# Softmax of the later attention tiles head by head on ScalarE, and the quarter-product weights formed at other places of a one-core kernel

## The chip, the core and the metric

The kernel runs on one core of one Trainium2 chip. The metric is the time of one launch in device microseconds, the median of some runs. One execution was taken by the hardware profiler, and all rows below are of that one.

## The reference

Everything is float32. The input is attention over independent chunks of 64 positions (8 batches, 8 heads, 576 positions, 64 numbers each), then two layers over 4608 tokens:

```python
scores = scale * np.matmul(q_c, k_c.transpose(0, 1, 2, 4, 3))   # 64 x 64 per chunk
attn = np.exp(scores - np.max(scores, axis=-1, keepdims=True))
attn = attn / (np.sum(attn, axis=-1, keepdims=True) + 1e-09)
x = np.matmul(attn, v_c)                                        # laid out as 4608 x 512
x = softplus(x @ w_in) @ w_out                                  # 512 -> 2048 -> 512
h = np.maximum(np.maximum(x @ w1, x @ w2), x @ w3)              # 512 -> 768
out = h @ w_out2                                                # 768 -> 512
```

The weights come as float64 and are split on the chip into float32 parts.

## The kernel before, in words

**Blocks and tiles.** The 4608 tokens are 9 blocks of 512. A block has 4 attention tiles (two heads each), 36 in all. Tiles 0 to 7 are made by `attention_first`, tiles 8 to 35 by `attention`, which is the function that the change is about. A float32 matmul is done in three passes over a high and a low part, so each operand is split: a cast makes the high part (g or s), and a subtraction on VectorE makes the low one (`cut_up`, or the pair `copy_op` and `tt_op`; on the profile lines 281, 283 and 288, which are the helpers).

**Stages.** Blocks 0 to 2 go through the first layer in plain steps (`mlp1`). Blocks 3 to 8 go in three pairs: `strassen()` runs eight `UnitA` per pair, each of seven half-size products p1 to p7 where eight would be plain, and then the second half of the layer, the outs. For pairs 0 and 1 these are `mlp1_out` steps of both blocks (the block that comes later reloads its g from DRAM, `tmp<-gd`), for pair 2 the quarter products of `Sevens.step` (steps p = 5, 6, 3, 4, 7, four each). The last layers are three `Triple`, each of 15 products per width (`product`, line 1558) and the outs (line 1656).

**What `attention` does for a tile.** It loads q and k in a shape that VectorE can transpose (lines 689 and 690), and v. A group of 64x64 matmuls makes the scores of this tile and the weighted sum of an older one. For 14 tiles (8 to 21) the group stands among the `mlp1` steps and writes the PSUM tile `aps`. For the other 14 (22 to 35, `apart`) it stands behind p7 of a unit (line 588 on the profile) and writes the two banks X and Z (`one` on the profile), which p2, and p5 and p3, of the units write too. Then comes `softmax`: the maximum of each head's 64 scores (line 545 or 563), the subtraction (line 288, `p<-one,mx` or `p<-aps,mx`), one activation over 512 numbers (line 579; Softplus with a shift of -20 stands for the exponential), the sums (line 580), two tiny operations, the division, a transpose (line 742), and a trip through DRAM (`pd`).

**Weights.** `combos` forms the weights of the quarter products: from four wide weight tiles of the first layer it makes four sums and four combinations, splits each combination, and stores them with six GpSimd DMAs into `wso`. It is called four times, for n2 = 0 to 3. `weights3(late)` does the like for the Triples, with stores into `w2c`, and `Triple.product` loads them (line 1541). `againa` loads the unit weights (`s<-wac`, line 1034).

**What sets the order.** All engines run lists that `Plan.order` writes before the launch: it takes every operation with its cost per engine and its due time (an operation without one gets the earliest of those that need it, less their cost), and at each moment gives an idle engine the ready operation that is due first. So an engine's list is fixed, and an operation that waits holds up all behind it on that engine. The matmuls of the pairs are chained in program order (`in_line("h", ...)`), so their order is fixed by the program. GpSimd (POOL) and SyncE (SP) issue most DMAs and also work through fixed lists.

The places where the change acts are `softmax` (line 535), its call in `attention` (line 739), `put` in `weights3` (line 903), the table `COMBOS` (line 977), the gate of the `w2c` loads (line 1544) and the calls of `combos` (line 1771):

```python
COMBOS = (1, 4, 7, 10)          # after which outs of pair 0
MORE = (3, 0), (5, 0), (5, 0)   # after which steps of the quarter products
```

Of the kernel before, what the change touches and what calls it, by code (L numbers as in the profile page):

```python
# [10 lines left out]
F32 = mybir.dt.float32  # L11
# [3 lines left out]
AF = mybir.ActivationFunctionType  # L15
# [5 lines left out]
P = 128  # L21
# [162 lines left out]
def tile_kernel(ctx: ExitStack, tc: tile.TileContext, q, k, v, w_in, w_out, w1, w2, w3, wo2, out):  # L184
# [350 lines left out]
    def softmax(sc, pbuf, by_head=False):  # L535
# [4 lines left out]
        if sc is None:  # L540
            s3 = lambda e: XZ.t[e][:, :TB // 2].rearrange("p (c k) -> p c k", k=CH)
            for h in range(2):
# [6 lines left out]
                )  # L549
            for h in range(2):  # L550
# [10 lines left out]
        else:  # L561
            s4 = lambda: sc.t[:, :, :TB // 2].rearrange("p e (c k) -> p e c k", k=CH)
            op({"D": 0.69}, lambda e: nc.vector.reduce_max(m4(), s4(), axis=AX.X), r=[(sc, "s")], w=[mx], alloc=[mx, sm])
            if by_head:
                op({"D": 0.1}, lambda e: nc.vector.tensor_scalar(mx.t, mx.t, -SCALE, -DROP, ALU.mult, ALU.add), w=[mx])

                def heads(e):
                    for u in range(H):
                        nc.scalar.activation(
                            p3()[:, u], s4()[:, u // HP, u % HP], AF.Softplus, bias=mx.t[:, u:u + 1], scale=SCALE  # L570
                        )

                op({"A": 1.9}, heads, r=[(sc, "s"), mx], w=[pbuf], alloc=[pbuf])
            else:
                tt_op(
                    p4, s4, lambda: m4()[:, :, :, None].to_broadcast([P, 2, HP, CH]), ALU.subtract, [(sc, "s"), mx], [pbuf], alloc=[pbuf]
                )
        if not by_head:
            op({"A": 0.62}, lambda e: nc.scalar.activation(pbuf.t, pbuf.t, AF.Softplus, bias=drop[:, :1], scale=SCALE), w=[pbuf])
        op({"D": 0.69}, lambda e: nc.vector.reduce_sum(sm.t, p3(), axis=AX.X), r=[pbuf], w=[sm])  # L580
# [95 lines left out]
    def attention(t, after=(), apart=False):  # L676
# [62 lines left out]
        softmax(None if apart else G, pbuf)  # L739
# [131 lines left out]
    def weights3(late, after):  # L871
# [31 lines left out]
        def put(s, r):  # L903
# [9 lines left out]
            tt_op(lo, view(r), lambda: hi().bitcast(F32), ALU.subtract, keys(r) + [(zs[0], "h")], [(zs[-1], "l")], n=n1, hold=[token])  # L913
# [63 lines left out]
    COMBOS = (1, 4, 7, 10)  # L977
# [114 lines left out]
    class UnitA:  # L1092
# [88 lines left out]
        def p3(u):  # L1181
            u.product(3, lambda: two("Z", TB), False, w=[(XZ, "Z")])
            u.add("Z", 0, 1)
# [295 lines left out]
    class Triple:  # L1479
# [47 lines left out]
        def product(u, s, d, alloc=()):  # L1527
# [8 lines left out]
            else:  # L1536
                zs, rings = [slot("w", "x") for _ in range(1 + late)], [Buf("ringb") for _ in range(1 + late)]
                for k, z in enumerate(zs):
# [5 lines left out]
                        after=[store["c", s, late + k], mark["step", *MORE[0]]],  # L1544
# [145 lines left out]
    def strassen():  # L1690
# [19 lines left out]
        for q in range(pairs):  # L1710
# [7 lines left out]
            for n, m in enumerate(ORDER[q]):  # L1718
# [3 lines left out]
                mark["unit", q, n] = begin  # L1722
                if n == SEVENS_LOAD and sevens:
                    mark["sevens", q] = begin
# [43 lines left out]
            for j in range(NJ - 2):  # L1768
                o = out()
                if q == 0 and j in COMBOS:  # L1770
                    combos(COMBOS.index(j), [o], clock[0] + 15.0)
# [113 lines left out]
```

## Time and profile before

| what | value |
|---|---|
| median of 3 runs (lowest, highest) | 1369.16 us (1365.87, 1371.52) |
| the profiled execution, its own time | 1368.65 us |
| its span | 1366.8 us |
| TensorE matmul busy (PE) | 1331.3 us, 97% |
| VectorE busy (DVE) | 1002.6 us, 73% |
| ScalarE busy (ACT) | 505.8 us, 37% |
| GpSimd busy (POOL) | 323.9 us, 24% |
| mean granted TensorE clock | 0.996 of full speed |

The span runs from the first to the last instruction; the time of the launch has 1.85 us around it. A share of busy time is a mean over stages that have different limits. The matmuls take nearly the whole span, so what can be gained is what stands between them.

### The profile page before, as it was taken

The numbers are of one execution on the slowest core, as the hardware profiler recorded it, in microseconds if no ns is written. First come the engines' busy times: TensorE is split into PE (matmuls) and PEld (weight loads), VectorE is DVE, ScalarE is ACT, GpSimd is POOL, SyncE is SP. The second block draws the span as 40 slices with busy tenths as digits, with TensorE's granted clock in tenths as the row PEclk, the third lists the DMA queues.
The fourth block names the chain that finished last, engine by engine and source line by source line (L and its number), as shares of the span: only waits on it lengthen the run. The fifth ranks groups of instructions, "written<-read, shape, count | busy, mean of one in ns | idle before, by whom it ended". The sixth has DMA issues, their size and how long they took to land.

```text
span 1366.8 us, 22719 instructions
## 1 busy us (share of the span) xinstructions
PE 1331.3 (97%) x8616; PEld 1091.1 (80%) x8616; DVE 1002.6 (73%) x1551; ACT 505.8 (37%) x793; POOL 323.9 (24%) x568
## 2 busy tenths in 40 slices
PE   5899999999999999999999999999999999999998
PEld 3788888888888778777788887888888888888886
DVE  8999976797676998658958897879714597145951
ACT  4544333354433544335535553432123222132211
POOL 2011545542233324323231122121101122011100
PEclk9899999999999999999999999999999999999999
DMA  8655567676788999887886799655644465344301
GB/s 273 172 165 156 126 194 202 192 261 212 202 246 258 286 327 294 266 282 257 337 296 223 249 345 364 232 192 208 212 149 162 139 231 202 143 147 154 139 30 63
DMA packets 220253, 293.56 MB, mean 215 GB/s; under 512 B 121984, under 2 KB 147008, under 8 KB 220144
## 3 DMA queue, kind: packets, MB, share of 16 engines
q0 software_dynamic: 54400, 180.31, 38.3%
q1 hardware_dynamic: 164928, 111.02, 27.0%
q8 instruction: 68, 1.11, 0.3%
q10 hardware_dynamic: 816, 0.79, 0.2%
q14 instruction: 41, 0.34, 0.1%
HBM read 198.71 MB, written 93.32 MB: 214 GB/s over the span
## 4 chain that ended last, share of the span: by engine, by line
PE 86%; DMA 6%; DVE 5%; SPq 2%; issue 1%; ACT 0%; POOL 0%; DVEq 0%; ACTq 0%; POOLq 0%
PE acc L1558 14%; PE both L1558 13%; PE acc L816 9%; PE acc L1410 9%; PE ph L796 9%; PE ph L1109 8%; PE one L1109 6%; PE both L1656 6%; PE acc L1656 5%; PE acc L1330 2%; PE acc L1263 2%; DVE s L288 2%; DMA rk<-in_k_dram 1%; PE ph L1330 1%; PE aps L503 1%
## 5 line engine op out<-in xcount | busy, mean ns | idle before, releaser
L288 DVE TENSOR_TENSOR s<-s,s 128x1024 fp32r<-128x1024 f32 (+3 forms) x216 | 208.7, 990 | 24.9 <-ACT s L281 11.7
L1410 PE MATMUL acc<-g,s 128*128 128x512 f32 x768 | 184.8, 393 | 3.7 <-DVE g L288 3.7
L1410 PEld LDWEIGHTS acc<-g,s 128*128 128x128 f32 x768 | 142.6, 188 | 35.8 <-DVE g L288 5.8
L1109 PE MATMUL ph<-s,s 128*128 128x512 f32 x576 | 144.3, 390 | 3.0 <-DMA s<-wac 2.1
L796 PE MATMUL ph<-s,s 128*128 128x512 f32 x576 | 141.2, 396 | 0.0
L816 PE MATMUL acc<-g,s 128*128 128x512 f32 x576 | 139.6, 391 | 0.0
L1109 PEld LDWEIGHTS ph<-s,s 128*128 128x128 f32 x576 | 107.9, 188 | 26.2 <-DMA s<-wac 2.6
L796 PEld LDWEIGHTS ph<-s,s 128*128 128x128 f32 x576 | 108.8, 190 | 23.4
L816 PEld LDWEIGHTS acc<-g,s 128*128 128x128 f32 x576 | 107.4, 188 | 22.7
L1541 POOL DMA_DIRECT2D s<-w2c x105 | 55.9, 532 | 278.1 <-PE both L1558 87.5
L281 ACT CAST g<-s 128x1024 fp32r<-128x1024 f32 (+1 forms) x68 | 62.2, 914 | 159.8 <-PE both L1558 36.3
L1558 PE MATMUL acc<-s,s 128*128 128x512 f32 x452 | 120.3, 389 | 0.0
L281 ACT CAST s<-s 128x512 fp32r<-128x512 f32 (+1 forms) x100 | 82.1, 832 | 91.5 <-DVE s L288 32.2
L1558 PE MATMUL acc<-g,s 128*128 128x512 f32 x400 | 110.0, 389 | 0.0
L1109 PE MATMUL one<-s,s 128*128 128x512 f32 x432 | 106.6, 390 | 1.2 <-DVE tmp L288 0.7
L1558 PE MATMUL both<-s,s 128*128 128x512 f32 x400 | 106.3, 389 | 0.0
L1558 PE MATMUL both<-g,s 128*128 128x512 f32 x368 | 100.1, 389 | 0.0
L1558 PEld LDWEIGHTS acc<-s,s 128*128 128x128 f32 x452 | 84.9, 188 | 17.6
L1109 PEld LDWEIGHTS one<-s,s 128*128 128x128 f32 x432 | 80.9, 188 | 19.1 <-DVE tmp L288 1.5
L288 DVE TENSOR_TENSOR g<-tmp,g 128x512 fp32r<-128x512 f32 x104 | 71.1, 684 | 33.2 <-ACT g L281 33.1
L468 POOL DMA_DIRECT2D rv<-in_v_dram x102 | 62.1, 613 | 115.4 <-issue 53.6
L1558 PEld LDWEIGHTS both<-s,s 128*128 128x128 f32 x400 | 75.1, 188 | 15.6
(157 smaller groups left out, 2103.9 us busy)
## 6 DMA issues: line engine op xcount, KB each, us to landing
s<-w2c POOLq DMA_DIRECT2D x105, 512.0 KB, 4.4
s<-wac POOLq DMA_DIRECT2D x66, 512.0 KB, 6.5
w2c<-s POOLq DMA_DIRECT2D x45, 512.0 KB, 4.3
wac<-s POOLq DMA_DIRECT2D x24, 512.0 KB, 5.6
s<-wso SPq DMA_DIRECT2D x20, 512.0 KB, 7.2
s<-in_moe_w_dram POOLq DMA_DIRECT2D x18, 512.0 KB, 4.9
s<-x2d POOLq DMA_DIRECT2D x18, 512.0 KB, 5.6
s<-in_moe_w_in_dram SPq DMA_DIRECT2D x16, 512.0 KB, 5.1
```

What stands on the lines that cost most here:

```text
L281: nc.scalar.copy(dst(), src())
L288: return op({"D": 0.69 * n}, lambda e: nc.vector.tensor_tensor(dst(), a(), b(), f), r=r, w=w, **kw)
L468: dma(out=dst().rearrange("p (c e d) -> p c e d", e=2, d=D)[half * CH:(half + 1) * CH, lo:lo + mine, h, :], in_=v[b, t % HP * 2 + h].rearr ...
L796: nc.tensor.matmul(ph.t, w[:, wi, kk * P:(kk + 1) * P], x[kk].t[:, xi], start=(kk == 0 and wi == 0 and xi == 0), stop=(kk == KD - 1 and wi ...
L816: nc.tensor.matmul(acc[m // 2].t[:, m % 2], w[:, wi, m * P:(m + 1) * P], g.t[:, gi, :], start=(first and wi == 0 and gi == 0), stop=(last ...
L1109: nc.tensor.matmul(dst(), ws.t[:, wi, col + kk * P:col + (kk + 1) * P], x[kk].t[:, xi], start=(first and kk == 0 and wi == 0 and xi == 0), ...
L1263: nc.tensor.matmul(u.acc[f].t[:, m], w.t[:, wi, m * P:(m + 1) * P], g.t[:, gi, :], start=(first and wi == 0 and gi == 0), stop=(last and w ...
L1330: nc.tensor.matmul(dst(m), z.t[:, wi, nn * HT + m * P:nn * HT + (m + 1) * P], (GH, GL)[gi].t[:, nn], start=(fresh and nn == 0 and wi == 0 ...
L1410: nc.tensor.matmul(acc[half].t[:, m % 2], w.t[:, wi, m * P:(m + 1) * P], g.t[:, gi, :], start=(first and wi == 0 and gi == 0), stop=(last ...
L1541: lambda e, k=k, z=z: nc.gpsimd.dma_start(out=z.t.bitcast(F32), in_=w2c[s][late + k]),
L1558: nc.tensor.matmul(bank.view()[:, f], ws(wi, slice(f * HT + kk * P, f * HT + (kk + 1) * P)), (XH, XL)[xi].t[:, kk], start=(first and kk == ...
L1656: nc.tensor.matmul(banks[t // 2].view()[:, t % 2], (GH, GL)[gi].t[:, f, t * P:(t + 1) * P], wo2_of[j].t[:, wi], start=(j == 0 and wi == 0 ...
```

## The change

There are five edits.

1. `softmax` gets a switch `sums`, and `attention` calls it with `by_head` and `sums` on. For tiles 8 to 35 the subtraction and the sums on VectorE go. A tiny operation scales the maxima, and eight activations of 64 numbers read the scores straight from PSUM, take the maximum off as their bias, and give the sum of their row as a second output. `attention_first` is called as before.
2. `combos` is called behind the out 2 of pair 0 (n2 = 0) and behind the first product of the units 0, 3 and 6 of pair 1 (n2 = 1, 2, 3), where all four stood behind the outs 1, 4, 7 and 10 of pair 0. Its due time is 30 us behind the call instead of 15.
3. The low parts in `weights3(0)` get a due time of their own.
4. The `w2c` loads of the first Triple from product 2 on wait for the first step of quarter product 7, not of 3.
5. The planner's cost of the activations is 2.6 with sums, 1.9 without.

```diff
-    def softmax(sc, pbuf, by_head=False):
+    def softmax(sc, pbuf, by_head=False, sums=False):
...
+            r = [(XZ, "X"), (XZ, "Z")]
+            one = lambda u: s3(u // HP)[:, u % HP]
+        else:
+            s4 = lambda: sc.t[:, :, :TB // 2].rearrange("p e (c k) -> p e c k", k=CH)
+            op({"D": 0.69}, lambda e: nc.vector.reduce_max(m4(), s4(), axis=AX.X), r=[(sc, "s")], w=[mx], alloc=[mx, sm])
+            r = [(sc, "s")]
+            one = lambda u: s4()[:, u // HP, u % HP]
+        if by_head:
+            op({"D": 0.1}, lambda e: nc.vector.tensor_scalar(mx.t, mx.t, -SCALE, -DROP, ALU.mult, ALU.add), w=[mx])
+
+            def heads(e):
+                for u in range(H):
+                    nc.scalar.activation(
+                        p3()[:, u],
+                        one(u),
+                        AF.Softplus,
+                        bias=mx.t[:, u:u + 1],
+                        scale=SCALE,
+                        accum_out=sm.t[:, u:u + 1] if sums else None,
+                    )
+
+            op({"A": 2.6 if sums else 1.9}, heads, r=[*r, mx], w=[pbuf, sm] if sums else [pbuf], alloc=[pbuf])
+        elif sc is None:
...
-        op({"D": 0.69}, lambda e: nc.vector.reduce_sum(sm.t, p3(), axis=AX.X), r=[pbuf], w=[sm])
+        if not sums:
+            op({"D": 0.69}, lambda e: nc.vector.reduce_sum(sm.t, p3(), axis=AX.X), r=[pbuf], w=[sm])
...
-        softmax(None if apart else G, pbuf)
+        softmax(None if apart else G, pbuf, True, True)
...
-            tt_op(lo, view(r), lambda: hi().bitcast(F32), ALU.subtract, keys(r) + [(zs[0], "h")], [(zs[-1], "l")], n=n1, hold=[token])
+            tt_op(lo, view(r), lambda: hi().bitcast(F32), ALU.subtract, keys(r) + [(zs[0], "h")], [(zs[-1], "l")], n=n1, hold=[token], due=None if late else T0 + STEP * NJ * (NP + 4))
...
-    COMBOS = (1, 4, 7, 10)
+    COMBOS = (("out", 0, 2), ("unit", 1, 0), ("unit", 1, 3), ("unit", 1, 6))
+    LATER = (7, 0)
...
-                        after=[store["c", s, late + k], mark["step", *MORE[0]]],
+                        after=[store["c", s, late + k], mark["step", *(MORE[0] if s < 2 or u.q else LATER)]],
...
+                if ("unit", q, n) in COMBOS:
+                    combos(COMBOS.index(("unit", q, n)), [begin], clock[0] + 30.0)
...
-                if q == 0 and j in COMBOS:
-                    combos(COMBOS.index(j), [o], clock[0] + 15.0)
+                if ("out", q, j) in COMBOS:
+                    combos(COMBOS.index(("out", q, j)), [o], clock[0] + 30.0)
```

How the lists move. On the engines' lists the lines of the changed kernel carry its own line numbers (9 or 10 higher behind `softmax`). The matmul list is the same row by row up to the first `mlp1` steps, and all of its later differences are places of 64x64 groups among the steps and, in the quarter products, other tiles for the same factors.

VectorE, in the outs of pair 0 behind the score group of unit 7. Before (s_244 and s_245 are the sums of `combos` for n2 = 1, tmp_78 its first combination, g the low parts that the outs wait for):

```order
L288 TENSOR_TENSOR p_89<-one_4129,mx_71 128x256
L288 TENSOR_TENSOR s_244_5634<-s_57_1342 128x512
L288 TENSOR_TENSOR p_89<-one_4130,mx_71 128x256
L288 TENSOR_TENSOR s_244_5634<-s_67_1536 128x512
L288 TENSOR_TENSOR s_245_5635<-s_62_1448 128x512
L288 TENSOR_TENSOR s_245_5635<-s_72_1602 128x512
L288 TENSOR_TENSOR g_77<-tmp_85,g_77 128x512
L288 TENSOR_TENSOR tmp_78<-s_244_5634,s_245_5635 128x512
```

The same outs in the change, up to where the sums for n2 = 1 (here s_250) begin:

```order
L288 TENSOR_TENSOR g_77<-tmp_83,g_77 128x512
L698 STREAM_TRANSPOSE s_248_5860<-rq_74 128x512
L288 TENSOR_TENSOR g_76<-tmp_86,g_76 128x512
L288 TENSOR_TENSOR g_75<-tmp_82,g_75 128x512
L288 TENSOR_TENSOR g_77<-tmp_80,g_77 128x512
L288 TENSOR_TENSOR g_76<-tmp_85,g_76 128x512
L288 TENSOR_TENSOR s_250_5918<-s_57_1342 128x512
```

The combinations for n2 = 1 now stand behind the last low parts of these outs; those for 2 and 3 stand among the units of pair 1. Between the two additions of p2 and p5 that enclose these outs VectorE's list had 78 operations and now has 58.

VectorE again, the score group behind unit 4 of pair 1. Before (`one_4129` and `one_4130` are the banks X and Z):

```order
L545 TENSOR_REDUCE mx_73<-one_4129 128x4
L689 STREAM_TRANSPOSE s_299_6651<-rq_74 128x512
L545 TENSOR_REDUCE mx_73<-one_4130 128x4
L288 TENSOR_TENSOR p_89<-one_4129,mx_73 128x256
L690 STREAM_TRANSPOSE s_299_6651<-rk_87 128x512
L288 TENSOR_TENSOR p_89<-one_4130,mx_73 128x256
```

Now (line 558 is the tiny operation, behind which ScalarE reads both banks):

```order
L698 STREAM_TRANSPOSE s_293_6754<-rq_74 128x512
L545 TENSOR_REDUCE mx_73<-one_4215 128x4
L288 TENSOR_TENSOR g_75<-tmp_81,g_75 128x512
L545 TENSOR_REDUCE mx_73<-one_4216 128x4
L332 TENSOR_SCALAR tmp_78<-s_287_6655 128x512
L558 TENSOR_SCALAR mx_73<-mx_73 128x8
L699 STREAM_TRANSPOSE s_293_6754<-rk_87 128x512
```

The transpose of k no longer stands ahead of the last operation on VectorE that the banks need.

GpSimd, in the quarter products. Before (`w2c_0_183`, `186`, `189` ... are the loads of products 0, 1, 2 ...):

```order
L1541 DMA s_461_8500<-w2c_0_183 128x1024
L917 DMA w2c_1_187<-s_462_8503 128x1024
L917 DMA w2c_2_188<-s_463_8504 128x1024
L1541 DMA s_467_8544<-w2c_0_186 128x1024
L1541 DMA s_471_8569<-w2c_0_189 128x1024
L1541 DMA s_475_8602<-w2c_0_192 128x1024
```

Now:

```order
L1551 DMA s_461_8654<-w2c_0_183 128x1024
L926 DMA w2c_1_187<-s_462_8657 128x1024
L926 DMA w2c_2_188<-s_463_8658 128x1024
L1551 DMA s_465_8680<-w2c_0_186 128x1024
L926 DMA w2c_1_190<-s_473_8740 128x1024
L926 DMA w2c_2_191<-s_474_8741 128x1024
L926 DMA w2c_1_193<-s_478_8776 128x1024
L926 DMA w2c_2_194<-s_479_8777 128x1024
L1551 DMA s_483_8838<-w2c_0_189 128x1024
```

The load of product 2 stands four stores later.

## Rows read from the trace of the kernel before

**Rows 1.** The page's first line.

```profile
span 1366.8 us, 22719 instructions
```

**Rows 2.** Windows: stretch, length, PE PEld DVE ACT POOL busy, clock, DMA share, GB/s.

```profile
0.00:68.00 68.00, 47.46 (x1290) 37.68 (x1291) 61.57 (x138) 34.00 (x79) 8.13 (x19) 0.92 0.75 222
...
460.00:502.00 42.00, 38.72 (x226) 30.65 (x225) 39.35 (x71) 19.92 (x35) 14.67 (x24) 1.00 0.93 324
502.00:619.00 117.00, 113.67 (x847) 91.98 (x846) 84.28 (x161) 49.43 (x90) 39.10 (x66) 1.00 0.90 277
619.00:684.00 65.00, 63.69 (x336) 51.64 (x335) 57.36 (x101) 33.59 (x61) 16.51 (x29) 1.00 0.84 300
...
sum 1264.00, PE 1253.94 PEld 1029.04 DVE 934.65 ACT 466.38 POOL 315.72; mean PE 156.74 PEld 128.63 DVE 116.83 ACT 58.30 POOL 39.47
...
1332.00:1366.80 34.80, 29.87 (x132) 24.41 (x130) 6.35 (x7) 5.41 (x7) 0.00 (x0) 0.99 0.18 70
```

**Rows 3.** Waits of PE from 68 to 1332 us: total, times, longest.

```profile
PE acc L1410 <- DVE g L288: 3.7, 4, 2.2
PE ph L1109 <- DMA s<-wac: 2.1, 1, 2.1
PE acc L1330 <- DVE s L288: 1.0, 1, 1.0
PE ph L1109 <- ACT tmp L281: 0.9, 1, 0.9
PE one L1109 <- DVE tmp L288: 0.7, 1, 0.7
```

**Rows 4.** Groups by line and form: busy us, mean ns, idle before, releasers.

```profile
L579 ACT ACTIVATE p<-p,drop 128x512 f32<-128x512 f32 x28 | 20.3, 725 | 64.0 <-DVE p L288 64.0
L569 ACT ACTIVATE tmp<-acc,mx 128x64 f32<-128x64 f32 x32 | 7.0, 330 | 5.0 <-DVE mx L565 4.9
L288 DVE TENSOR_TENSOR p<-one,mx 128x256 f32<-128x256 f32 x28 | 11.3, 413 | 0.2 <-ACT s L281 0.2
L288 DVE TENSOR_TENSOR p<-aps,mx 128x512 f32<-128x512 f32 x14 | 9.4, 669 | 0.0
L580 DVE TENSOR_REDUCE mx<-p 128x8 f32<-128x512 f32 x28 | 19.0, 678 | 3.7 <-ACT p L579 3.7
L288 DVE TENSOR_TENSOR g<-tmp,g 128x512 fp32r<-128x512 f32 x104 | 71.1, 684 | 33.2 <-ACT g L281 33.1
L565 DVE TENSOR_SCALAR mx<-mx 128x8 f32<-128x8 f32 x4 | 0.7, 172 | 0.0
```

**Rows 5.** Timeline, the longest wait in the outs of pair 0.

```profile
497.39 1.89 DVE L288 TENSOR_TENSOR s<-s 128x512 f32<-128x512 f32 x3
...
499.19 0.69 DVE L288 TENSOR_TENSOR g<-tmp,g 128x512 fp32r<-128x512 f32 x1
...
499.94 2.79 PE L1410 MATMUL acc<-g,s 128*128 128x512 f32 x11 [2.23 <-DVE g L288]
```

**Rows 6.** Timeline, the score group behind unit 4 of pair 1.

```profile
584.63 0.65 PE L588 MATMUL one<-s 64*64 64x64 f32 x32
...
586.06 0.42 DVE L545 TENSOR_REDUCE mx<-one 128x4 f32<-128x256 f32 x1
...
588.77 0.71 DVE L689 STREAM_TRANSPOSE s<-rq 128x512 f32<-128x512 f32 x1 [2.29 <-DMA rq<-in_q_dram]
...
591.69 0.71 DVE L690 STREAM_TRANSPOSE s<-rk 128x512 f32<-128x512 f32 x1 [1.56 <-DMA rk<-in_k_dram]
592.32 0.39 DVE L288 TENSOR_TENSOR p<-one,mx 128x256 f32<-128x256 f32 x1
...
592.81 1.63 PE L1109 MATMUL one<-s,s 128*128 128x512 f32 x6 [0.51 <-issue]
```

**Rows 7.** Timeline, two waits in the quarter products.

```profile
823.03 1.23 DVE L288 TENSOR_TENSOR s<-s,s 128x1024 f32<-128x1024 f32 x1 [1.65 <-DMA s<-w2d]
...
834.12 2.11 PE L1330 MATMUL acc<-g,s 128*128 128x512 f32 x8 [0.22 <-DVE g L288]
```

More of the change, by code (lines that the diff above doesn't have):

```diff
@@ L561, in softmax @@
         else:
[L562 to L577, printed above, removed]
+            tt_op(p4, s4, lambda: m4()[:, :, :, None].to_broadcast([P, 2, HP, CH]), ALU.subtract, [(sc, "s"), mx], [pbuf], alloc=[pbuf])
         if not by_head:
             op({"A": 0.62}, lambda e: nc.scalar.activation(pbuf.t, pbuf.t, AF.Softplus, bias=drop[:, :1], scale=SCALE), w=[pbuf])
-        op({"D": 0.69}, lambda e: nc.vector.reduce_sum(sm.t, p3(), axis=AX.X), r=[pbuf], w=[sm])
+        if not sums:
+            op({"D": 0.69}, lambda e: nc.vector.reduce_sum(sm.t, p3(), axis=AX.X), r=[pbuf], w=[sm])
         op({"D": 0.1}, lambda e: nc.vector.tensor_scalar(sm.t, sm.t, 1e-9 * float(np.exp(-DROP)), None, ALU.add), w=[sm])
```

## The prediction

> **What bounds the kernel now.** I read the busy times first: the matmuls are busy for 1331.3 us (the table above) of the span's 1366.8 us [rows 1], so the 35.5 us in which PE stands idle are all that other engines can give back. The windows say where these are [rows 2]: 68.00 - 47.46 = 20.5 us lie before 68 us, while the first tiles and weights come in, and 34.80 - 29.87 = 4.9 us at the end, where the last results leave. Between 68 and 1332 us it is 1264.00 - 1253.94 = 10.1 us. The granted clock is 1.00 in the three stretches that matter, so no matmul gets faster there. The lists of matmuls and of VectorE for the first 68 us are the old ones, and nothing of the end is touched. What the change can win is therefore at most 10.1 us, or 0.7%; what it can lose has no such bound. A measurement of this kernel can tell about 0.5%, or 6.8 us, from no change.
>
> The waits of PE say who is late [rows 3]: 3.7 us the low parts g on VectorE, 2.1 us a weight load, 1.0 us VectorE in the quarter products, 0.9 us a copy on ScalarE, 0.7 us an addition on VectorE. The rest are some tenths each. VectorE is full in one of these places: from 460 to 502 us, where PE is idle for 42.00 - 38.72 = 3.3 us, it is busy for 39.35 of 42 us [rows 2]. From 502 to 619 us, with 3.3 us of idle PE too, it has 84.28 of 117 us, and DMA is at 0.90; there it is latency that is late, not work.
>
> **The softmax.** On VectorE a tile of the banks X and Z loses two subtractions, 11.3 / 14 = 0.81 us, and the sums, 19.0 / 28 = 0.68 us, and gets a tiny operation of 0.17 us: 1.32 us less [rows 4]. A tile of `aps` loses 9.4 / 14 = 0.67 us and 0.68 us, and gets 0.17 us: 1.18 us less. That is 14 x 1.32 + 14 x 1.18 = 35 us over the program, all of it beside the matmuls. ScalarE loses 0.73 us a tile, and eight activations of 64 numbers come. Without sums the trace has them: 7.0 / 32 = 0.22 us each where they overlap, 0.33 us each by their mean duration [rows 4]. With sums it has none. The near bound is 8 x 0.22 = 1.75 us a tile (a second output for nothing); the far one is a second activation for the sum, 8 x 0.66 = 5.3 us. I take 8 x 0.33 = 2.6 us, no overlap, since a sum must be handed on before the next row starts. That is +1.9 us a tile, 28 x 1.9 = 53 us on an engine that is idle for two thirds of the span, in place of its 64.0 us of waits for the subtraction [rows 4].
>
> The *Trainium skill* speaks against this edit: "ScalarE: Activation LUTs", Rules for kernel authors, says to use VectorE, not ScalarE, for maxima, additions and products. The rows agree on the price (1.9 us bought with 1.3 us); by the rule alone the edit would cost 28 x 0.6 = 17 us of engine time, and by the rows none of it is on the path while ScalarE waits anyway.
>
> What counts is when the banks X and Z come free. Behind unit 4 of pair 1 the group ends at 584.63 + 0.65 = 585.3 us, and PE writes a bank again at 592.81 us after a wait of 0.51 us [rows 6]: it can be late by 7.0 us for nothing. Before, the bank is free with the second subtraction (592.32 us). There the transposes of q and k stand between the maxima and the subtractions, and each waits for its load, 2.29 and 1.56 us. In the new list the one of k stands behind the tiny operation. With q as late as before, the first maximum starts at 589.4 us, a low part (0.68 us), the second maximum (0.4 us), one more operation (0.4 us) and the tiny one follow, and the eight activations begin near 591.2 us: free at 591.2 + 1.75 = 593.0 or 591.2 + 2.6 = 593.8 us. So the wait of 0.5 us here stays about as it is. In the group before, behind unit 3, no transpose stands there any more. For the waits on k, I count 0.5 us won: the two waits of 0.5 and 0.7 us at this place (the row of 592.81 us and the addition of [rows 3]) hang on the same late load. The bounds are 1.2 us won and, were the banks late by 1 us at all 13 groups that a unit follows, 13 us lost.
>
> **The combinations.** One call has twelve operations of 512 numbers on VectorE, 0.6 us apart when they follow each other (three take 1.89 us where one takes 0.69 [rows 5]; 12 x 0.6 = 7.2 us), four casts, and six stores of 2.5 MB in all. Four calls are 29 us in the outs of pair 0, in the stretch where VectorE has 39.35 of 42 us. In the new list 58 operations stand there instead of 78, about 12 us less, and the sums for n2 = 1 begin behind the low parts. VectorE then has some 27 of 42 us. The longest wait, 2.23 us, is for a g that starts at 499.19 us [rows 5] behind three sums of `combos`. I count all 3.3 us of this stretch as won; the bounds are 3.3 and 0, if the reloads of g and not VectorE are late.
>
> Three calls move to the units of pair 1. VectorE gets 2.5 x 7.2 - 6 x 1.32 = 10 us more from 502 to 619 us: 94 of 117 us; from 619 to 684 us some 4 us more: 61 of 65 us. Full it is not, and the operations are due 30 us later, so g goes first. I count nothing for the matmuls, with bounds of 0 and +3 us (as in the stretch that is full now). The due time in `weights3(0)` I count at nothing: it is hidden by the same matmuls, and what it costs is in that bound.
>
> Each moved call also puts six stores into GpSimd's list among the unit weights. A store that waits for its combination holds up the loads behind it. The trace has one late load there, 2.1 us [rows 3]. I count that wait as staying; it could go (2.1 us won) or come three times (6.3 us lost).
>
> **The gate of the `w2c` loads.** In the quarter products PE waits 1.0 us [rows 3] for a low part that stands behind an operation for which VectorE waited 1.65 us on a `w2d` load [rows 7]. This load was issued before any `w2c` load of product 2, and VectorE's list up to there is the old one, so this wait stays. The 0.22 us at 834 us may go. I count 0.2 us won, with bounds of 1.7 us won (all three waits of 0.5, 1.0 and 0.2 us) and 2 us lost, if product 2's own load, four stores further back, comes late.
>
> **The sum.** 3.3 + 0.5 + 0.2 = 4.0 us won. Against the profiled execution's own 1368.65 us that is 1364.65 us; the median of the runs shown is 0.5 us above that execution, so I say **1365.1 us**.
>
> **The rivals.**
> *All waits go.* VectorE has 35 us less to do, the outs of pair 0 lose 5 MB of stores, and if the late loads of k and of the unit weights were late because of that traffic, the 10.1 us go: 1369.2 - 10.1 = 1359.1 us. For it: DMA is at 0.93 up to 502 us. Against it: it is at 0.90 and 0.84 behind [rows 2], and the stores now go there.
> *The wait only moves.* Unit weights behind waiting stores, a load like that of 2.1 us in each of the three units: -4.0 + 6.3, or 1371.5 us. For it: the lists show stores and loads mixed. Against it: stores of 0.5 MB are quick where their operands are ready.
> *Slower: the sums take a second pass.* If an activation with a sum takes 0.66 us, the banks are held for 5.3 us. From the end of a group to the last maximum and the tiny operation it is at least 0.4 + 0.68 + 0.4 + 0.68 + 0.17 = 2.3 us, and 0.8 us went by before the first maximum began (585.3 to 586.06 us [rows 6]): 8.4 us against the 7.0 that PE gives. That is 1.4 us at each of 13 groups, 18 us, less the 4.0: 1383 us. It decides from (7.0 - 3.1) / 8 = 0.49 us an activation. Against it: the edit asks for the sum in the same instruction.
> The *Trainium skill* has the rule behind this rival: "Perfetto Trace Analysis", Matmuls, says that matmul groups should rotate through PSUM banks, so that one is emptied while the next is filled. X and Z have no second copy; by the rule every group costs a wait, by the rows [rows 6] only one that is emptied later than 7.0 us.
>
> **How the numbers follow.** The forecast has 0.52, all waits go 0.19, the wait moves 0.19, the second pass 0.08, and 0.02 are for what I don't see. Below 1362.3 us (faster by over 0.5%) are the second case and a tenth of the first: 0.24. Above 1376.0 us are the second pass, a tenth of the third case and the rest: 0.12. Within it is 0.64. The range reaches from 1358.5 us, just below all waits gone, to 1373.0 us, above the moved wait: some 0.1 lies on either side.
>
> **What would show it.** Right: VectorE well below 39 of 42 us in the outs of pair 0, and no wait for g there; the new activations at 0.3 us or less; X and Z written no later than 0.5 us after PE could. Wrong: waits of PE for ScalarE at `one`, new waits for `wac` behind unit 3 or 6, or the g waits of pair 0 still there with VectorE idle, which would put them on the reloads.

## The result: slower by 0.75%, and the profile after

The changed kernel takes 1380.66 us (median, 1377.01 to 1383.04) where the kernel before takes 1370.35 us on the same chip: a ratio of 1.0075, 95% interval 1.0052 to 1.0099. The forecast was 1365.1 us, in a range of 1358.5 to 1373.0. The execution profiled took 12.1 us more between its first and last instruction. The page's first line and its line of PE, of the changed kernel:

```profile
span 1378.9 us, 23115 instructions
...
PE 1335.3 (97%) x8616; PEld 1095.9 (79%) x8616; DVE 983.1 (71%) x1531; ACT 540.4 (39%) x1191; POOL 326.5 (24%) x569
```

Of the 12.1 us, 4.0 are more matmul time (1335.3 against 1331.3 us, for the same 8616 matmuls) and 8.1 are idle PE (43.6 against 35.5 us). The windows of [rows 2], after, with two whole stretches below:

```profile
460.00:502.00 42.00, 42.00 (x244) 34.65 (x245) 33.73 (x61) 19.36 (x46) 10.37 (x17) 1.00 0.94 290
502.00:619.00 117.00, 111.05 (x833) 90.69 (x832) 81.25 (x157) 54.92 (x159) 41.30 (x68) 0.99 0.85 263
619.00:684.00 65.00, 60.09 (x309) 48.30 (x308) 50.94 (x90) 32.06 (x71) 16.39 (x28) 0.95 0.85 304
684.00:790.00 106.00, 103.14 (x448) 84.94 (x447) 81.21 (x132) 49.61 (x83) 22.14 (x39) 0.98 0.75 260
```

```profile
68.00:1332.00 1264.00, 1247.26 (x7146) 1024.64 (x7145) 912.63 (x1384) 499.31 (x1102) 318.33 (x550) 0.99 0.67 219
1332.00:1378.90 46.90, 40.29 (x178) 33.06 (x176) 8.87 (x10) 6.57 (x9) 0.00 (x0) 0.96 0.18 68
```

Before 68 us PE idles for 20.3 us (20.5 before), up to 1332 us for 1264.00 - 1247.26 = 16.7 us (10.1 before), at the end for 6.6 us (4.9 before). The outs of pair 0 (460 to 502 us) are full now, 42.00 of 42 us, and VectorE has room there: 33.73 us. The loss is behind them: from 502 to 684 us PE idles for 10.9 us where it idled for 4.6, and the granted clock, 1.00 before, is 0.99 and 0.95, then 0.98.

The matmuls of the pairs have the same order in both kernels, so the groups of 64x64 matmuls show where the time went (timelines of the group behind unit 3 of pair 1 and of the last group, the changed kernel first, then the kernel before):

```profile
560.40 0.70 PE L597 MATMUL one<-s,rv 64*64 64x64 f32 x32
...
655.98 0.69 PE L597 MATMUL one<-s,rv 64*64 64x64 f32 x32
```

```profile
567.56 0.69 PE L588 MATMUL one<-s,rv 64*64 64x64 f32 x32
...
649.97 0.69 PE L588 MATMUL one<-s,rv 64*64 64x64 f32 x32
```

At the first of them the change is 7.2 us ahead, at the second 6.0 us behind, at the end 12.1 us. So gains like those forecast did come, and 13 us were lost in the 96 us between the two groups. PE's waits, which answer to [rows 3]:

```profile
PE acc L1420 <- DVE g L288: 5.0, 2, 4.7
PE ph L1119 <- DMA s<-wac: 4.9, 1, 4.9
PE ph L1119 <- ACT tmp L281: 2.9, 1, 2.9
PE acc L1340 <- DVE s L288: 1.2, 1, 1.2
PE ph L1340 <- DVE g L288: 1.2, 1, 1.2
```

Two waits of nearly 5 us, and one of 2.9, make up most of it. **The first** ends at 586.93 us, in the units of pair 1 (timeline of the changed kernel, PE, VectorE and GpSimd):

```profile
573.30 0.54 POOL L1241 DMA_DIRECT2D wso<-s  x1
...
575.23 0.71 DVE L751 STREAM_TRANSPOSE s<-p 128x512 f32<-128x512 f32 x1 [3.79 <-DMA wso<-s]
...
577.77 0.73 PE L597 MATMUL one<-s,rv 64*64 64x64 f32 x29 [1.01 <-DVE tmp L288]
...
579.21 0.54 POOL L1044 DMA_DIRECT2D s<-wac  x1 [3.23 <-PE one L597]
...
580.49 0.53 POOL L1044 DMA_DIRECT2D s<-wac  x1 [0.74 <-issue]
...
582.89 1.26 POOL L1044 DMA_DIRECT2D s<-wac  x2 [1.87 <-issue]
...
586.93 2.93 PE L1119 MATMUL ph<-s,s 128*128 128x512 f32 x6 [4.94 <-DMA s<-wac]
```

VectorE stands still for 3.79 us before a transpose of the attention, released by a store of combined weights (`wso<-s`); I read that as the transpose writing a buffer that the store had still to read. The next addition in its list frees a bank, so the group of 64x64 matmuls starts 1.01 us late.

That delay is small beside the 4.94 us. PE waits for the unit weights whose load is issued at 579.21 us and lands 7.7 us later. The row gives the end of the group as what released this load. But in the run wso_small, described below, every engine has the same list, and there the same load starts before that group (timeline, GpSimd; the group starts at 576.56 us there):

```profile
573.97 0.67 POOL L1044 DMA_DIRECT2D s<-wac  x1
577.76 1.59 POOL L1044 DMA_DIRECT2D s<-wac  x3 [3.13 <-PE one L597]
```

What fits is GpSimd's own queue. The loads at 579.21, 580.49 and 582.89 us each start 0.3 us after an earlier transfer of this queue has landed: those issued at 572.76, 573.30 (a store of combined weights) and 574.15 us took 6.1, 6.9 and 8.4 us. From 500 to 700 us GpSimd has 51 waits of over 0.5 us before a transfer, and 31 of them end 0.28 to 0.37 us after such a landing. That GpSimd waits for room in its queue is my reading; for most of these waits the profile names no releaser.

**The second** ends at 642.58 us:

```profile
630.94 0.76 POOL L318 DMA_DIRECT2D s<-in_moe_w_dram  x1 [5.32 <-DVE g L288]
...
631.69 0.56 POOL L1241 DMA_DIRECT2D wso<-s  x1
...
632.96 0.54 POOL L1241 DMA_DIRECT2D wso<-s  x1
...
639.55 0.43 DVE L332 TENSOR_SCALAR tmp<-s 128x512 int32<-128x512 int32 x1 [6.70 <-DMA s<-in_moe_w_dram]
...
641.85 0.68 DVE L288 TENSOR_TENSOR g<-tmp,g 128x512 fp32r<-128x512 f32 x1
...
642.58 3.78 PE L1420 MATMUL acc<-g,s 128*128 128x512 f32 x8 [4.67 <-DVE g L288]
```

VectorE waits 6.70 us for expert weights. Their load is issued at 630.94 us, again 0.3 us after an earlier one (624.85 us, 5.7 us to land), and takes 8.6 us to land, with two stores of combined weights issued right behind it; the low part g that PE needs stands behind that wait in VectorE's list. No engine is short of time in either place: VectorE has 81.25 of 117 us and 50.94 of 65 us, less than before. The engines work through fixed lists, and one instruction that waits for a transfer holds what stands behind it.

**The third**, of 2.86 us, ends at 691.04 us and is for a copy on ScalarE. Before, the wait for such a copy was 0.9 us [rows 3]; why it grew is open.

**The clock** is the rest. The granted clock was at about half at the end of the first two waits and from 692.2 us, 1.2 us behind the end of the third, and stayed there for 3 to 5 us of matmuls. That is the lower of its two levels (1.2 of 2.4 GHz). After the 2.23 us wait of the kernel before [rows 5] it stayed at 1.00. Windows, of the changed kernel and of the kernel before:

```profile
586.90:590.00 3.10, 3.07 (x8) 2.48 (x9) 2.09 (x5) 0.10 (x1) 0.63 (x1) 0.53 1.07 340
642.58:647.90 5.32, 5.32 (x13) 4.16 (x14) 5.32 (x11) 1.78 (x4) 1.26 (x2) 0.50 1.00 362
692.20:695.70 3.50, 3.50 (x10) 2.74 (x9) 0.10 (x1) 0.58 (x1) 0.19 (x1) 0.51 0.49 152
```

```profile
499.94:502.00 2.06, 2.06 (x9) 1.72 (x10) 2.06 (x4) 0.62 (x1) 0.00 (x0) 1.00 0.25 99
```

The *Trainium skill*, "TensorE: Matmul & The Clock Gate", What's actually happening, says that the array's clock is throttled by default and that activity releases it; these rows agree, 0.50 to 0.53 behind 4.9, 4.7 and 2.9 us without a matmul. The 31 matmuls of these rows took 11.9 us; at the 29.87 / 132 = 0.226 us a matmul of the last stretch of [rows 2] they would take 7.0 us, so the half clock cost some 5 us, an estimate, beside the 4.0 us more of matmul time.

The length of one wait does not settle whether the clock falls. In g_only, one of the runs below, a wait of 2.23 us that ended at 506.59 us, as long as that of [rows 5], was followed by half clock; in null_after27 one of 3.05 us that ended at 693.75 us was not (1.00 from there to 698 us). The window of g_only:

```profile
507.90:511.30 3.40, 3.40 (x10) 2.63 (x9) 2.83 (x5) 0.60 (x2) 1.20 (x2) 0.50 0.28 108
```

**The softmax** takes about the time that was forecast. Groups by line and form, which answer to [rows 4]:

```profile
L562 ACT ACTIVATE p<-one,mx 128x64 f32<-128x64 f32 x112 | 33.3, 324 | 20.0 <-DVE mx L558 20.0
...
L562 ACT ACTIVATION_READ_ACCUMULATOR p<-one,mx 128x1 f32 x112 | 24.3, 217 | 0.0
```

An activation with a sum is two instructions, but they overlap. The first of the eight of one tile, in the timeline:

```profile
583.14 0.31 ACT L562 ACTIVATE p<-one,mx 128x64 f32<-128x64 f32 x1 [3.23 <-DVE mx L558]
583.36 0.19 ACT L562 ACTIVATION_READ_ACCUMULATOR p<-one,mx 128x1 f32 x1
```

One starts every 0.29 us, and a tile takes 2.47 us (the median of the 28 tiles; 583.14 to 585.61 here), against 2.6 us forecast. The banks X and Z are free 4.1 to 6.6 us after the end of each of the 14 groups that have their softmax here, and PE writes one of them again 6.86 us after that end at the earliest: never late, and PE has no wait for ScalarE at `one`.

### The profile page after: what moved, and what is told of

Same layout as the page of the kernel before. It is cut to its first block, busy times and chain, and to the rows that moved or that the text cites. A ratio compares the mean times of both kernels' runs of the same rounds, so it can differ in the third digit from the quotient of the medians.

```text
span 1378.9 us, 23115 instructions
## 1 busy us (share of the span) xinstructions
PE 1335.3 (97%) x8616; PEld 1095.9 (79%) x8616; DVE 983.1 (71%) x1531; ACT 540.4 (39%) x1191; POOL 326.5 (24%) x569
## 4 chain that ended last, share of the span: by engine, by line
PE 80%; DVE 6%; DMA 5%; issue 5%; POOL 2%; SPq 1%; ACT 1%; POOLq 0%; DVEq 0%; ACTq 0%
PE acc L1568 14%; PE both L1568 13%; PE acc L825 8%; PE acc L1420 8%; PE ph L805 8%; PE ph L1119 8%; PE both L1666 6%; PE one L1119 6%; PE acc L1666 5%; DVE s L288 2%; PE acc L1340 2%; PE acc L1273 1%; DMA s<-w2d 1%; DMA s<-wac 1%; PE aps L503 1%
## 5 line engine op out<-in xcount | busy, mean ns | idle before, releaser
L1420 PEld LDWEIGHTS acc<-g,s 128*128 128x128 f32 x768 | 145.8, 192 | 37.1 <-DVE g L288 5.9
L825 PEld LDWEIGHTS acc<-g,s 128*128 128x128 f32 x576 | 107.3, 188 | 23.0 <-DVE g L288 0.4
L1568 PEld LDWEIGHTS acc<-g,s 128*128 128x128 f32 x400 | 75.1, 188 | 15.5
```

The source lines that it names most:

```text
L825: nc.tensor.matmul(acc[m // 2].t[:, m % 2], w[:, wi, m * P:(m + 1) * P], g.t[:, gi, :], start=(first and wi == 0 and gi == 0), stop=(last ...
L1420: nc.tensor.matmul(acc[half].t[:, m % 2], w.t[:, wi, m * P:(m + 1) * P], g.t[:, gi, :], start=(first and wi == 0 and gi == 0), stop=(last ...
L1568: nc.tensor.matmul(bank.view()[:, f], ws(wi, slice(f * HT + kk * P, f * HT + (kk + 1) * P)), (XH, XL)[xi].t[:, kk], start=(first and kk == ...
```

## The experiments

Three theories stood against each other. **A**: the moved combinations cost the time, since their stores (`wso`) stand among the loads of pair 1. **B**: the softmax does, with 4.3 us on ScalarE a tile (the two instructions added up). **C**: any edit makes new lists, and each set of lists has its own collisions of an engine that works in order with a transfer that is late.

### The edits apart

The five edits were switched alone and together: S is the softmax (edits 1 and 5), M the moved combinations (edit 2), G the two gates (edits 3 and 4). The diff of each is the part of the change that it names; the rest is as before.

s_only, S alone:

> Kernel before with the softmax edit alone (ScalarE takes the maximum off and sums, combinations where they were, gates as they were). Theory A, the moved combinations cost the time (their stores stand among the loads of pair 1): no stall over 2.5 us in 500-700 us, span 1363 to 1370. Theory B, the softmax costs it (8 x (0.32 + 0.22) = 4.3 us of ScalarE a tile where 2.6 was assumed): stalls before bank X or Z or before the mlp1 copies, span 1374 to 1383. Theory C, any edit shuffles the planned lists and the stalls fall anywhere: a span anywhere in 1360 to 1380, with stalls at places that neither edit touches.

c_only, M alone:

> Kernel before with the combinations moved alone (softmax and gates as before). Theory A: stalls of some 3 to 5 us at a wac load or at a g combination in pair 1, span 1375 to 1383. Theory B: 1361 to 1369, the g waits of the outs of pair 0 gone. Theory C: anywhere in 1360 to 1380.

sg_no_c, S and G:

> Changed kernel with the combinations put back to outs 1, 4, 7 and 10 of pair 0 and their due time to 15 us. Theory A: 1363 to 1370, g waits of 2 to 4 us back in the outs of pair 0, no long stall in pair 1. Theory B: 1376 to 1384. Theory C: anywhere in 1360 to 1380.

cg_no_s, M and G:

> Changed kernel with the softmax of before (VectorE takes the maximum off and sums). Theory A: 1376 to 1383, with the stalls of pair 1. Theory B: 1361 to 1368. Theory C: anywhere in 1360 to 1380.

g_only, G alone:

> Kernel before with the two gate edits alone (due time of the first split, later gate for the second loads). Prediction's terms: -0.2 and 0, so 1368 to 1371 beside 1369. If the lists it reshuffles cost what the changed kernel without the moved combinations lost against the softmax edit alone (3.8 us): 1372 to 1374.

sc_no_g, S and M:

> Changed kernel without the two gate edits (softmax edit and moved combinations stay). If the moved combinations cost of themselves: 1372 to 1388. If the gate edits cost what they did alone (7.8 us): 1366 to 1374.

| edits | run | median us | ratio to before, 95% interval |
|---|---|---|---|
| S | s_only | 1367.10 | 0.9987 (0.9972 to 1.0001) |
| G | g_only | 1376.46 | 1.0061 (1.0042 to 1.0081) |
| S, G | sg_no_c | 1370.88 | 1.0024 (1.0006 to 1.0043) |
| M | c_only | 1388.50 | 1.0152 (1.0132 to 1.0171) |
| S, M | sc_no_g | 1377.50 | 1.0065 (1.0051 to 1.0078) |
| M, G | cg_no_s | 1387.13 | 1.0144 (1.0121 to 1.0167) |
| S, M, G | the change | 1380.66 | 1.0075 (1.0052 to 1.0099) |

B falls: a tile takes 2.47 us on ScalarE and not 4.3, s_only lies below B's 1374 to 1383 us, and in all four pairs that differ by S alone the kernel with S is faster, by 0.0013 (before and s_only, not clear of noise), 0.0037, 0.0087 and 0.0069. M makes it slower in all four pairs that differ by M alone, by 0.0152, 0.0078, 0.0083 and 0.0051. That is A's sign. But the same edit is worth three times as much in one pair as in another, and G, two gates counted at 0.2 us, costs 7.8 us alone, 0.0037 beside S, and almost nothing beside M (-0.0008 and +0.0010): C is in it too. c_only and cg_no_s came out above the ranges of all three theories, g_only above both of its own.

The stalls say how. In c_only VectorE waits 6.26 us at a cast for a store of combined weights, and the addition that frees a bank is behind it (timeline):

```profile
622.51 0.56 POOL L1241 DMA_DIRECT2D wso<-s  x1
...
629.01 0.43 DVE L283 CAST s<-tmp 128x512 fp32r<-128x512 f32 x1 [6.26 <-DMA wso<-s]
...
635.16 1.23 PE L597 MATMUL one<-s,rv 64*64 64x64 f32 x32 [7.23 <-DVE tmp L288]
```

In g_only, where nothing of pair 1's combinations is moved, ScalarE does the same at a cast that waits for a `w2c` store, with the copies of two results behind it (timeline; the profiled execution took 1381.57 us, 5 us more than the median):

```profile
653.68 0.62 ACT L281 CAST s<-s 128x512 fp32r<-128x512 f32 x1 [5.92 <-DMA w2c<-s]
...
654.21 1.06 ACT L281 COPY tmp<-acc 128x512 f32<-128x512 f32 x2
...
655.33 5.49 PE L1420 MATMUL acc<-g,s 128*128 128x512 f32 x12 [4.62 <-ACT tmp L281]
```

Even s_only has one such stall, at the banks, and a wait of PE for ScalarE at `one` is what the prediction named as a sign of being wrong: PE waits 4.19 us for the bank, since VectorE waits for a late load of k with the tiny operation behind the transpose (timeline):

```profile
557.25 0.71 DVE L699 STREAM_TRANSPOSE s<-rk 128x512 f32<-128x512 f32 x1 [3.88 <-DMA rk<-in_k_dram]
...
558.05 0.31 ACT L562 ACTIVATE p<-one,mx 128x64 f32<-128x64 f32 x1 [8.27 <-DVE mx L558]
...
560.59 1.94 PE L1119 MATMUL one<-s,s 128*128 128x512 f32 x4 [4.19 <-ACT p L562]
```

### The lists held still, the stores shrunk

wso_small has every engine's list as in the changed kernel. The stores of the combined weights carry 16 columns of 256, and the loads that read them later, in the quarter products, read other stored weights of the same size, so what the kernel leaves out is most of these stores' bytes:

```diff
-                        lambda e, w=w, nn=nn: nc.gpsimd.dma_start(out=wso[4][n2][:, :, nn, :], in_=w.t[:, :, HT:].bitcast(F32)),
+                        lambda e, w=w, nn=nn: nc.gpsimd.dma_start(out=wso[4][n2][:, :, nn, :16], in_=w.t[:, :, HT:HT + 16].bitcast(F32)),
...
-                lambda e: nc.gpsimd.dma_start(out=wso[p][n2].rearrange("p w n c -> p w (n c)"), in_=z.t.bitcast(F32)),
+                lambda e: nc.gpsimd.dma_start(out=wso[p][n2].rearrange("p w n c -> p w (n c)")[:, :, :16], in_=z.t[:, :, :16].bitcast(F32)),
...
-                lambda e: nc.sync.dma_start(out=z.t.bitcast(F32), in_=wso[at][n2].rearrange("p w n c -> p w (n c)")),
+                lambda e: nc.sync.dma_start(out=z.t.bitcast(F32), in_=wac[2 * n2][at % 3]),
```

> Changed kernel, every engine's list the same, but the stores of the combined weights carry 16 of 256 columns (and their later loads read other stored weights of the same size), so the third quarter products are not the reference's: what is left out is the stores' traffic. Theory A1 (a store of 512 KB takes 6 to 7 us to land where the planner counted about 4, and VectorE, whose list is fixed, stands still for it): the 4.9 us and 4.7 us stalls at 582 and 638 us shrink below 1.5 us, 1366 to 1372. Rival A2 (the order of VectorE's and ScalarE's lists in pair 1 is what stalls, whatever the stores do): 1377 to 1383, the stalls stay.

It took 1371.07 us, 1.0023 (1.0007 to 1.0040), where the change has 1.0075: 0.0052, or 7 of the 10 us lost, go with the stores' bytes, as A1 expected. In the profiled execution, which at 1366.82 us lies 4 us under the median, PE is busy for all 117.00 us from 502 to 619 us (windows) and waits for no unit weight there; the wait that answers to the second one is 0.55 us. From 619 to 684 us PE still idles for 6.1 us, most of it in three other waits of 1.5 to 2.1 us, where the change idles for 4.9 us. VectorE does the same instructions without the wait of 3.79 us (timeline):

```profile
502.00:619.00 117.00, 117.00 (x866) 96.01 (x866) 86.64 (x167) 59.01 (x178) 44.94 (x72) 1.00 0.75 231
619.00:684.00 65.00, 58.92 (x306) 47.10 (x305) 53.82 (x92) 33.94 (x62) 17.07 (x29) 0.97 0.81 302
```

```profile
570.56 0.69 DVE L288 TENSOR_TENSOR tmp<-one,tmp 128x512 f32<-128x512 f32 x1
571.16 0.70 DVE L751 STREAM_TRANSPOSE s<-p 128x512 f32<-128x512 f32 x1
```

So in the change's own lists the bytes of the stores are the cause of most of the loss, as A says. The stores, of the change from 500 to 690 us and then of this run from 500 to 700 us (queue, KB each, median us from issue to landing):

```profile
wso<-s POOLq DMA_DIRECT2D x12, 512.0 KB, 7.0
```

```profile
wso<-s POOLq DMA_DIRECT2D x16, 16.0 KB, 4.2
```

A store of 512 KB took 7.0 us to land. The planner counts 1.0 + 2.2 + 0.8 = 4.0 us for one that starts on an empty queue. The *Trainium skill*, "DMA: Bandwidth & Descriptors", Anatomy of one DMA, has a fit that gives 2.0 + 0.524 / 0.436 = 3.2 us for this size, an estimate for a transfer by itself; beside the loads of pair 1 the measured one is twice that. The 16 KB stores still took 4.2 us.

c_small does the same to c_only's lists:

> Moved combinations alone, every engine's list the same as in that run, but the stores of the combined weights carry 16 of 256 columns (their later loads read other stored weights), so the third quarter products are not the reference's. A1: the 7.2 us stall at 628 us (VectorE behind a store's landing) goes, the 7.2 us one at 876 us stays: 1376 to 1381. If the stores have no part: 1386 to 1390.

It took 1384.47 us, 1.0121 (1.0102 to 1.0141), so it missed: some 4 us of the 19 came back, and the two intervals overlap. Its stall at 628 us only fell from 7.23 to 5.96 us, because VectorE still waited 5.0 us for a 16 KB store, and the one of 7.23 us at 876 us stayed. That store was issued at 626.23 us, behind a 512 KB load of 625.46 us, and took 5.2 us to land, 0.9 us after the load. In these lists the bytes are a small part; that a store stands behind a large load, and just before the cast that needs its buffer, is enough.

### Other draws of the same work

null_before and null_after change one number that only the planner reads, so each engine has the same work in another order; null_after27 does it the other way:

```diff
-            op({"A": 0.62}, lambda e: nc.scalar.activation(pbuf.t, pbuf.t, AF.Softplus, bias=drop[:, :1], scale=SCALE), w=[pbuf])
+            op({"A": 0.73}, lambda e: nc.scalar.activation(pbuf.t, pbuf.t, AF.Softplus, bias=drop[:, :1], scale=SCALE), w=[pbuf])
...
-            op({"A": 2.6 if sums else 1.9}, heads, r=[*r, mx], w=[pbuf, sm] if sums else [pbuf], alloc=[pbuf])
+            op({"A": 2.5 if sums else 1.9}, heads, r=[*r, mx], w=[pbuf, sm] if sums else [pbuf], alloc=[pbuf])
```

> Kernel before, same work, one number of the planner changed: the softmax activation is costed at 0.73 us, which it takes, instead of 0.62. Theory C (each new set of lists draws its own collisions of an in-order engine with a late transfer): a shift of 2 to 8 us either way, with stalls at places of their own. Theory A alone (only the moved stores cost): within 2 us of before.

> Changed kernel, same work, the summing activations costed at 2.5 us a tile, which they take, instead of 2.6. Theory C: anywhere in 1370 to 1388. Theory A alone: the stores stand where they stood, so 1378 to 1383.

> Changed kernel, same work, the summing activations costed at 2.7 us instead of 2.6. Theory C: anywhere in 1368 to 1388. If the moved combinations cost of themselves: 1376 to 1388.

null_before took 1384.20 us, 1.0103 (1.0085 to 1.0120): 13 us lost by a more truthful number. null_after took 1372.15 us, 1.0013 (1.0000 to 1.0025): 8.5 us won back. null_after27 took 1378.15 us, 1.0070 (1.0050 to 1.0090). So C is shown: a draw alone moved this kernel by up to 13.4 us, where only the two runs with M and without S lost more. That is outside the 2 to 8 us put down for null_before. More than half of what null_before lost is one stall of 7.5 us, in the first Triple, where a copy on ScalarE starts only when VectorE is through some five of seven additions (timeline; that the copy waits for a buffer that they read is my reading, the profile names no releaser):

```profile
877.28 8.15 DVE L288 TENSOR_TENSOR s<-s,s 128x1024 f32<-128x1024 f32 x7
883.40 1.01 ACT L281 COPY s<-acc 128x1024 f32<-128x1024 f32 x1 [9.88 <-issue]
...
884.46 5.29 PE L1568 MATMUL acc<-s,s 128*128 128x512 f32 x12 [7.50 <-ACT s L281]
```

The number that was changed is not one of that place. c_only has the same stall (7.2 us at 876 us), a good part of its 19 us.

Five more draws changed what the planner is told or when the combinations are due. s_true and s_27 have S alone, at 2.5 and 2.7 us a tile; s_wso6 has S, and 6 us for the landing of the stores in `combos` where the planner had 2; wso_lat6 has the same in the changed kernel; due15 puts its due time back to 15 us.

```diff
-                lat=2.0,
+                lat=6.0,
...
-                    combos(COMBOS.index(("unit", q, n)), [begin], clock[0] + 30.0)
+                    combos(COMBOS.index(("unit", q, n)), [begin], clock[0] + 15.0)
```

> Changed kernel, the planner told 6 us instead of 2 for the landing of the stores of combined weights. A1: it puts other work before the next cast, no stall over 2 us in pair 1, 1362 to 1370. A2: lists are new, but pair 1 holds as much work as before: 1374 to 1383.

> Changed kernel with the combinations at their new places but due 15 us after their mark instead of 30. If the later due time lets them slip among pair 1's own loads: 1366 to 1373. If the place alone does it: 1377 to 1388.

> Softmax edit alone with 2.5 us a tile in the planner. If the edit itself is worth its 2 us: 1364 to 1369. Theory C: 1362 to 1377.

> Softmax edit alone, with the planner told 6 us for the landing of the stores of combined weights, whose casts then stand later. Theory A: 1360 to 1367, below the softmax edit alone. Theory C: 1362 to 1377.

> Softmax edit alone, the activations costed at 2.7 us a tile. If the moved combinations cost some 6 us of themselves, draws without them lie at 1366 to 1374: here too. If the draw is all: 1366 to 1384.

after_lat45 (the changed kernel) and s_lat45 (S alone) tell the planner 4.5 us instead of 2 for all loads and stores of split weights, and 2.5 us for the activations:

> Changed kernel with 2.5 us in the planner for the activations and 4.5 us instead of 2 for the landing of the weights' loads and stores (the traces have 4 to 7). If the collisions come from transfers taken as landed too soon: 1360 to 1367 and no stall over 2 us in pair 1. Theory C alone: 1366 to 1385.

> Softmax edit alone with 2.5 us for the activations and 4.5 us instead of 2 for the landing of the weights' loads and stores. If the collisions come from transfers taken as landed too soon: 1358 to 1365. Theory C alone: 1362 to 1378.

| S and the moved combinations | ratio | S without them | ratio |
|---|---|---|---|
| the change | 1.0075 | s_only | 0.9987 |
| null_after27 | 1.0070 | s_true | 0.9986 (0.9971 to 1.0001) |
| sc_no_g | 1.0065 | s_lat45 | 1.0015 (1.0000 to 1.0030) |
| due15 | 1.0064 (1.0044 to 1.0085) | s_wso6 | 1.0023 (1.0009 to 1.0036) |
| after_lat45 | 1.0045 (1.0024 to 1.0067) | sg_no_c | 1.0024 |
| wso_lat6 | 1.0043 (1.0026 to 1.0059) | s_27 | 1.0049 (1.0032 to 1.0066) |
| null_after | 1.0013 | | |
| mean of seven | 1.0054 | mean of six | 1.0014 |

The means differ by 0.0040, 5.4 us. The spread within a column is 0.0022 and 0.0024 (standard deviations), so the difference has a standard error of 0.0013. But the columns differ in the gates too: six of the seven on the left have G, and one of the six on the right. Without G it is sc_no_g at 1.0065 against a mean of 1.0012, with G a mean of 1.0052 against sg_no_c at 1.0024; each of these rests on a single run on one side. So the table alone shows some microseconds for M, and not how many.

The waits in the traces divide the runs more clearly. In all nine runs with M and whole stores VectorE waits for a `wso` store between 502 and 700 us, 3.4 to 6.3 us at the longest, and in eight of them PE waits for a unit weight (`wac`) there, 1.2 to 4.9 us (due15 has none). In the nine runs without M VectorE has no such wait there, and PE's wait for `wac` is 2.1 us in the kernel before, 0.7 us at most in the others. So the collision comes with the moved stores, whatever the draw, and the draw settles what it costs: null_after has it and is within 0.0013 of the kernel before.

Truer landing times did not make better lists: s_lat45 is no faster than s_true and lies above the 1358 to 1365 us put down for it, and after_lat45 misses its 1360 to 1367 us by over 7 us, with a 5.9 us wait of PE for ScalarE left at 648 us. wso_lat6 and due15 fell between the two ranges put down for each, and s_wso6 lies above A's. So the collisions are not settled by a larger constant.

The fastest are s_only and s_true, 0.9987 and 0.9986, with both intervals reaching 1.0001. The other three draws with S alone are slower than the kernel before, at 1.0015 to 1.0049. So a gain from the softmax alone isn't shown.

## Why the prediction was wrong

**Softmax: right in its price, in part by luck.** Forecast 2.6 us a tile, measured 2.47; the far bound, a second activation for the sum, is false, though a second instruction of 0.217 us is there. The reason given, that there is no overlap since a sum must be handed on before the next row starts, is not what the rows show: an activation and its read add up to 0.54 us, and one pair starts every 0.29 us. The rival of a second pass gave 1383 us, near what came out, but its condition (0.49 us an activation) was not met, at 0.29. The waits of 0.5 and 0.7 us at `one` [rows 3] are gone in the change; s_only got one of 4.19 us at the banks. What the 35 us taken from VectorE are worth stays open: the step counted 0.5 us, and the four pairs have 2 to 12 us (0.0013 to 0.0087), with the draws in them.

**Low parts in the outs of pair 0: right.** The 3.3 us of idle PE from 460 to 502 us are gone. VectorE was busy there for 33.73 us, where some 27 were forecast.

**The moved combinations: the step that failed.** Two terms were put at nothing: "I count nothing for the matmuls, with bounds of 0 and +3 us", and the late unit weight, "I count that wait as staying; it could go (2.1 us won) or come three times (6.3 us lost)". From 502 to 684 us the idle time grew by 10.86 - 4.64 = 6.2 us, more than the first bound, and against the same matmuls the change lost 13 us from 560 to 656 us.

The first term took VectorE's room (94 of 117 us) for safety; VectorE had even more, with 81.25 us busy. It reasoned that a later due time lets g go first. That holds only while the list is written. Once it is fixed, an operation that a late transfer releases holds g behind it, and the runs show such waits of VectorE: 6.70 us for expert weights in the change, and for stores 3.79 us in the change, 6.26 us in c_only and 4.98 us in c_small. The second term had the stores wait for their operands only. They took 7.0 us to land, and GpSimd's next loads started as the earlier transfers landed: one wait of 4.9 us for `wac`, where 2.1 us was the price of one.

"Stores of 0.5 MB are quick where their operands are ready" was thus the wrong argument against the second rival. That rival had the right place and kind, and new waits for `wac` were a sign of being wrong that the prediction named. That its 6.3 us stand beside 6.2 us of idle time is luck: three waits of 2.1 us were to come, and one of 4.9 us came, with one of 4.7 us for g. Its total, 1371.5 us, lies 9 us below the measured one.

**The clock: left out.** "The granted clock is 1.00" was read as a property of the stretch. Three waits were followed by half clock, for 11.9 us of matmuls; over the whole profiled execution the matmuls took 4.0 us more.

**The gates: 0.2 us counted.** The waits in the quarter products went from 1.7 us to 2.4 us ([rows 3, 7] and the waits above). Alone the gates cost 7.8 us, with the longest wait at a place that they were not weighed for (655 us); beside M they cost almost nothing.

**The range** was made of the bounds of single waits. A change of one planner number by 0.1 us moves this kernel by 13 us, so a range of 14.5 us was too narrow, above all towards slower, where the text itself says that there is no bound.

The 1.7 us more at the end (6.6 against 4.9 us) follow no edit: s_only has 5.1 us there and wso_small 6.7. Their cause is open. So is what makes up the 3 us that wso_small did not win back, and how the loss in c_only divides between the stall at 628 us and the one at 876 us, since they were not taken apart.

## What to carry to other kernels

Where a planner writes fixed lists, one timing of an edit is one draw: change a planner number that means nothing, see how far that moves the time, and judge the edit by several draws or with the lists held still and one transfer shrunk. Before moving work with stores into a stretch, look for the loads that stand behind the stores in the issuing engine's list, for the instructions that reuse the stored buffers, and for what stands behind those on their engine; the engine's busy share doesn't show it. To compare two profiles, take the times of the same matmuls: fixed windows hid here that the change was 7 us ahead before it lost 19. Price a stall with the clock behind it.

## What the hardware showed that was not expected

An activation with an accumulator output is followed by a read instruction of 0.217 us, but eight pairs take 2.47 us, not 8 x (0.32 + 0.22) = 4.3: their rows overlap. A 16 KB store on GpSimd's queue takes 4.2 us to land beside the loads of pair 1, against 7.0 us for 512 KB: a thirty-second of the bytes, more than half of the time. GpSimd's next transfers often start 0.3 us after an earlier one has landed (31 of 51 waits), so a slow store delays the issue of the loads behind it. Waits of 4.9, 4.7 and 2.9 us were followed by half clock; of two waits of 2.23 us one was and one was not, and one of 3.05 us was not.
